# A layer norm's steps moved between the stages of a fused attention and gated-MLP kernel

## The chip, the cores and the metric

The kernel runs on one core of one Trainium2 chip. The metric is the device time of one execution in microseconds (us), as the median of several runs. A core has five engines that run side by side, each with its own queue in order: TensorE (PE; its weight loads are shown as PEld), VectorE (DVE), ScalarE (ACT), GpSimd (POOL) and SyncE (SP), which here issues nearly all transfers (DMA). Matmuls write to PSUM, all else lies in SBUF.

## The reference

The input x has 2048 rows of 640 in bf16. The output is x plus attention of the normed rows plus a gated MLP of the same normed rows:

```python
x = A_x
xn = _layernorm(x, axis=-1)
return x + _A_ref(xn, A_wqkv, A_wo) + _B_ref(xn, B_w_gate, B_w_up, B_w_down)
```

Attention has 32 heads of 20 and a causal window of 256 keys. The MLP has a hidden width of 1536:

```python
scores = jnp.einsum("bhqd,bhkd->bhqk", q, k) * (Dh ** -0.5)
mask = (idx[:, None] - idx[None, :] >= 0) & (idx[:, None] - idx[None, :] < W)
p = _softmax(jnp.where(mask[None, None], scores, -1e9), axis=-1)
o = jnp.einsum("bhqk,bhkd->bhqd", p, v)

h = _sigmoid(x @ w_gate) * (x @ w_up)
return h @ w_down
```

## The kernel before

The 2048 rows are cut into four chunks of 512 (`NCH`), each into four blocks of 128 (`SBC`). The order of all engines is written out by the program (`manual_schedule`). A loop over attention steps (lines 760 to 782) issues the scores of a step (line 530), their exponentials (535), their masks on GpSimd (542) or as a MIN on VectorE (547), and, when a pair of groups of heads is complete, the weighted sums of V (561). Between those steps, `Fill` pulls pieces of other work from a list of named parts (lines 732 to 748), as much as a planned cost allows. The parts run strictly one after the other:

- `qk<c>`: ten blocks of the projections of chunk c, first five for Q, then five for K (`g_qk`, 334). VectorE copies the Q blocks out of PSUM (338), ScalarE the K blocks (340). SP stores each block to DRAM (342) and loads it back, spread by heads (352).
- `v<c>`: eight projections of V (`g_v`, 364); half of them are copied by VectorE (373). In `v1`, SP also loads the output weights wo here, twelve transfers (226, 228, 231).
- `gu<c>`: the gate and up projections (`g_gu`, 454 and 461), each with a tanh on ScalarE (457) and a product on VectorE (465) that gives h.
- `out<c>`: for each of four blocks the down projection (475), the output projection of attention (482), and on VectorE the sum with the rows of x (486) in SBUF; SP loads those rows (492) and stores the result (497). For block 0 and block 1 the loads are issued when the part begins, for later ones when the block before them begins. A part `out<c>` may start only when the attention of chunk c is done. Between the down projection of block 0 and its output projection it does some gate and up pieces.

All these projections use one PSUM pool, `ps_d`, of four buffers handed out in turn, as do the sums of V (561), which come in pairs and which VectorE transposes out (573) and scales (581 to 589).

What this is about is the layer norm of chunks 1 to 3 and its transposition. `g_norms(c)` is a generator. Each call of `next` does one step, and steps without cost (`yield 0`) only let time pass: statistics of four blocks on VectorE (271, 277), after the fourth one the reciprocal root on GpSimd (285, 286), four empty steps (the first is reached in the same call as the root), then four norms on VectorE (295), each with a store of the normed block to DRAM by SP (306). After the fourth store, `load_quarters` has SP read the whole chunk back from DRAM in four transfers, rearranged (313). These wait for the four stores to have landed. `g_turns(c)` then has VectorE transpose the four blocks (317) into xnT, which all projections of the chunk read. The chunk's rows, the rearranged rows and the next chunk's rows all use one buffer (`xc`), so that the next chunk is loaded (159) after the transposes.

`mix(a, b, first, every, rest)` yields the pieces of a and, after piece number `first` and every `every` pieces from there, one step of b. With `rest` true, what is left of b follows at the end.

Before the change, chunk 2's four statistics steps lie in the K half of `qk1`, and the rest (empty steps, norms, stores, quarters, waiting, transposes) in `out0`, a step after every piece from the second. Chunk 3's statistics lie in `gu1b`, the rest in `out1`. The x of chunk 3 is loaded between `out0` and `qk2`.

Of the kernel before, what the change touches and what calls it, by code (L numbers as in the profile page):

```python
# [112 lines left out]
def kernel(  # L113
# [42 lines left out]
    def load_x(c):  # L156
        t = xp.tile([P, SBC, D], BF16, name="xc")
        xc[c] = t
        nc.sync.dma_start(out=t, in_=xr[:, c * SBC:(c + 1) * SBC, :])
# [40 lines left out]
    def load_gu(t, w, k, lo=0, hi=FS):  # L200
        nc.sync.dma_start(out=t[k][:, :, lo:hi],
                          in_=w.rearrange("(c p) f -> p c f", p=P)[:, :, k * FS + lo:k * FS + hi])
# [20 lines left out]
    def load_wo():  # L223
        by_head = A_wo.rearrange("(a b i d) n -> a i b d n", a=2, i=HG, d=DH)
        for i in range(HG):
            nc.sync.dma_start(out=wo[32 * i:32 * i + DH, 0:DC - 1, :], in_=by_head[0, i].rearrange("b d n -> d b n"))
        for i in range(HG):
            nc.sync.dma_start(out=wo[32 * i + DH:32 * i + 32, 0:DC - 1, :],
                              in_=by_head[1, i].rearrange("b d n -> d b n")[0:32 - DH])
        for i in range(HG):  # L230
            nc.sync.dma_start(out=wo[32 * i:32 * i + 32, DC - 1, :], in_=by_head[1, i][:, 32 - DH:DH, :])
# [84 lines left out]
    def turn_block(c, s):  # L316
        nc.vector.transpose(out=xnT[c][:, :, s * P:(s + 1) * P],  # L317
                            in_=xc[c][:, s, :].rearrange("p (j b f) -> p b j f", j=SBC, b=DC))

    def new_xnT(c):  # L320
        xnT[c] = xtp.tile([P, DC, CW], BF16, name="xnT")
# [5 lines left out]
    def proj_block(w, c, m):  # L327


        base = 0 if w == "q" else D  # L330
        ps = ps_d.tile([P, CW], FP32, name="pqk", tag="d")
        for d in range(DC):
            wt = wqkv[:, d, base:base + D].rearrange("p (k m) -> p m k", m=DC)
            nc.tensor.matmul(ps, lhsT=wt[:, m, :], rhs=xnT[c][:, d, :],  # L334
                             start=(d == 0), stop=(d == DC - 1))
        st = stp.tile([P, CW], BF16, name="st")
        if w == "q":
            nc.vector.tensor_copy(out=st, in_=ps)
        else:
            nc.scalar.copy(out=st, in_=ps)  # L340
        dst = scratch[w].rearrange("(h j) s -> h j s", j=32)
        nc.sync.dma_start(out=dst[:, 4 * m:4 * m + 4, :], in_=st)

    def spread(w, c, g0, g1):

        half, first = divmod(g0, GH)
        if first == 0:
            qk[w, c, half] = (qp if w == "q" else kp).tile([P, GH, CW], BF16, name=w + "T")
        src = scratch[w].rearrange("(a b p) s -> b p a s", a=2, p=P)
        for b in range(g0 // 2, g1 // 2):  # L350
            o = 2 * b - half * GH
            nc.sync.dma_start(out=qk[w, c, half][:, o:o + 2, :], in_=src[b])

    def new_v(c, s):
        v = vp.tile([P, 2, VH], BF16, name="v")
        vt[c * SBC + s] = v
        nc.gpsimd.memset(v[:, :, 0:16 * VW].rearrange("p k (h d) -> p k h d", d=VW)[:, :, :, DH:VW], 0.5)
        nc.gpsimd.memset(v[:, :, 16 * VW:], 0.0)
# [17 lines left out]
    def proj_v(c, s, hf, copy):  # L376
        copy_v(c, s, hf, project_v(c, s, hf), copy)

    MM = 216
# [21 lines left out]
    def g_turns(c, wait=0):  # L401
        for _ in range(wait):
            yield 0
        new_xnT(c)
        for s in range(SBC):
            turn_block(c, s)
            yield 0

    def g_qk(c):
        for w in "qk":  # L410
            for m in range(DC):
                proj_block(w, c, m)
                if c == 0 and w == "q" and m == 1:
                    load_x(1)
                if c == 0 and w == "q" and m == 3:
                    load_gu(wu, B_w_up, 0, FS // 2)
                if c and w == "k" and m == 1:
                    spread("q", c, 0, GH)
                yield 5 * MM
        if c == 0:  # L420
            spread("q", c, 0, 2)
            spread("k", c, 0, 2)
            spread("q", c, 2, 4)
            spread("k", c, 2, 4)

    def g_v(c):
        for s in range(SBC):
            new_v(c, s)
            for hf in range(2):
                proj_v(c, s, hf, nc.scalar.copy if hf else nc.vector.tensor_copy)  # L430
                if hf == 0:
                    yield 5 * 136
            if s == 0:
                spread("k", c, 0, 2)
                spread("k", c, 2, GH)
            if c == 1 and s == 2:
                load_wo()
            if s == 1:
                spread("q", c, GH, NG)
                spread("k", c, GH, NG)  # L440
            yield 5 * 136
# [4 lines left out]
    def part(w, d, f):  # L446
        k, first = divmod(f * P, FS)
        return w[k][:, d, first:first + P]

    def g_gu(c, f0, f1):  # L450
        for f in range(f0, f1):
            pg = ps_d.tile([P, CW], FP32, name="pg", tag="d")
            for d in range(DC):
                nc.tensor.matmul(pg, lhsT=part(wg, d, f), rhs=xnT[c][:, d, :],  # L454
                                 start=(d == 0), stop=(d == DC - 1))
            th = tp.tile([P, CW], FP32, name="th")
            nc.scalar.activation(out=th, in_=pg, func=TANH, scale=0.5)  # L457
            yield 5 * MM
            pu = ps_d.tile([P, CW], FP32, name="pu", tag="d")
            for d in range(DC):  # L460
                nc.tensor.matmul(pu, lhsT=part(wu, d, f), rhs=xnT[c][:, d, :],  # L461
                                 start=(d == 0), stop=(d == DC - 1))
            h = hp.tile([P, CW], BF16, name="h")
            ht[c, f] = h
            nc.vector.scalar_tensor_tensor(out=h, in0=th, scalar=1.0, in1=pu, op0=ADD, op1=MULT)  # L465
            yield 5 * MM
# [23 lines left out]
    def new_rows(c, s, name="rows", bufs=3, queue=nc.sync):  # L490
        rows = lnp.tile([P, D], BF16, name=name, bufs=bufs)
        queue.dma_start(out=rows, in_=xr[:, c * SBC + s, :])
        return rows
# [5 lines left out]
    def outp(c, s, ys, rows):  # L499
        for y, cut in zip(ys, HALVES):  # L500
            add_wo(c, s, y, cut)
        for y, cut in zip(ys, HALVES):
            add_x(y, cut, rows)
        store(c, s, rows)

    def g_out(c, between, ahead=()):
        nxt = new_rows(c, 0)
        for s in range(SBC):
            rows = nxt
            if s == 0:  # L510
                yield from ahead
            if s + 1 < SBC:
                nxt = new_rows(c, s + 1)
            ys = [ps_d.tile([P, CW], FP32, name=f"y{i}", tag="d") for i in range(2)]
            for y, cut in zip(ys, HALVES):
                yield from down(c, s, y, cut)
            if s == 0:
                yield from between
            outp(c, s, ys, rows)
            yield 10 * 136  # L520
# [115 lines left out]
    def mix(a, b, first, every=1, rest=True):  # L636

        for k, cost in enumerate(a):
            yield cost
            if k >= first and (k - first) % every == 0:  # L640
                yield next(b, 0)
        if rest:
            yield from b
# [75 lines left out]
    fill = Fill()  # L719
    GU = 10 * MM  # L720
    OUT = 4 * 34 * 136
# [5 lines left out]

    norms = {c: g_norms(c) for c in range(1, NCH)}
    first = itertools.chain(norms[1], g_turns(1, 8))
    second = itertools.chain(norms[2], g_turns(2, 5))  # L730
    third = itertools.chain(norms[3], g_turns(3, 5))
    fill.add("gu0a", mix(g_gu(0, 0, 4), first, 1, 1, False), 4 * GU)
    fill.add("gu0b", mix(g_gu(0, 4, 12), first, 0), 8 * GU)
    fill.add("wd", later(load_wd), 0)
    fill.add("x2", later(load_x, 2), 0)
    fill.add("qk1", mix(g_qk(1), second, 5, 1, False), 50 * MM)
    fill.add("v1", mix(g_v(1), g_gu(1, 0, 2), 1, 2), 40 * 136 + 2 * GU)
    fill.add("out0", mix(g_out(0, g_gu(1, 2, 3)), second, 1, 1), OUT + GU)
    fill.add("x3", later(load_x, 3), 0)
    fill.add("qk2", g_qk(2), 50 * MM)  # L740
    fill.add("v2", mix(g_v(2), g_gu(1, 3, 7), 0, 1), 40 * 136 + 4 * GU)
    fill.add("gu1b", mix(g_gu(1, 7, 12), third, 0, 2, False), 5 * GU)
    fill.add("out1", mix(g_out(1, g_gu(2, 0, 1)), third, 1, 1), OUT + GU)
    fill.add("qk3", g_qk(3), 50 * MM)
    fill.add("v3", mix(g_v(3), g_gu(2, 1, 5), 0, 1), 40 * 136 + 4 * GU)
    fill.add("gu2", g_gu(2, 5, 12), 7 * GU)
# [102 lines left out]
```

## Time and profile before

| | |
|---|---|
| median of 3 runs | 310.89 us (309.93 to 311.25) |
| the profiled execution | 310.85 us |
| its span, first to last instruction | 308.7 us |
| granted TensorE clock, mean | 1.000 |
| VectorE busy | 179.6 us |
| ScalarE busy | 198.3 us |
| GpSimd busy | 164.1 us |

The page's chain of work that ended last puts 87% on TensorE, 5% on VectorE and 4% on DMA. Its weightiest lines are the gate and up projections (16% each), Q and K (14%) and the down projection (14%). The stages around the change, in us from the span's start as their matmuls show in the timeline: `qk1` from 55.1, `v1` from 70.2, `out0` from 82.8, `qk2` from 108.2, `v2` from 122.1, `gu1b` from 139.8, `out1` from about 154. In a timeline each line has start, length, engine, line, operation, out<-in and how many were merged; in brackets stands how long the engine had been idle before, and what ended that.

A query of the busy time by stretches gives VectorE these shares (busy of length, us): 70 to 82: 9.06 of 12; 82 to 90: 7.67 of 8; 90 to 108: 10.30 of 18; 108 to 122: 9.15 of 14; 122 to 139: 10.07 of 17; 146 to 156: 8.75 of 10.

### The profile page before, as it was taken

The numbers are of one execution on the slowest core, as the hardware profiler recorded it, in microseconds if no ns is written. First come the engines' busy times: TensorE is split into PE (matmuls) and PEld (weight loads), VectorE is DVE, ScalarE is ACT, GpSimd is POOL, SyncE is SP. The second block draws the span as 40 slices with busy tenths as digits, with TensorE's granted clock in tenths as the row PEclk, the third lists the DMA queues.
The fourth block names the chain that finished last, engine by engine and source line by source line (L and its number), as shares of the span: only waits on it lengthen the run. The fifth ranks groups of instructions, "written<-read, shape, count | busy, mean of one in ns | idle before, by whom it ended". The sixth has DMA issues, their size and how long they took to land.

```text
span 308.7 us, 10027 instructions
## 1 busy us (share of the span) xinstructions
PE 300.8 (97%) x4309; PEld 168.1 (54%) x4344; DVE 179.6 (58%) x354; ACT 198.3 (64%) x196; POOL 164.1 (53%) x304
## 2 busy tenths in 40 slices
PE   7999999999999999999999999999999999999996
PEld 3654444555657655554456665554546665444775
DVE  4635657889684674485856755373643627372433
ACT  6933768688965647888655538978585557768100
POOL 3020667479874728576582827647383756657000
PEclk9999999999999999999999999999999999999999
DMA  7998969545746254630016313650000210000202
GB/s 208 365 292 266 319 212 287 150 137 151 213 150 114 61 180 130 196 115 0 2 46 148 91 57 92 196 171 0 4 0 4 67 41 23 2 2 2 87 23 65
DMA packets 40148, 36.04 MB, mean 117 GB/s; under 512 B 9000, under 2 KB 39848, under 8 KB 40104
## 3 DMA queue, kind: packets, MB, share of 16 engines
q1 hardware_dynamic: 39240, 34.63, 37.3%
q10 hardware_dynamic: 864, 0.77, 0.9%
q8 instruction: 34, 0.56, 0.8%
q14 instruction: 10, 0.08, 0.1%
HBM read 24.77 MB, written 10.62 MB: 115 GB/s over the span
## 4 chain that ended last, share of the span: by engine, by line
PE 87%; DVE 5%; DMA 4%; issue 1%; ACT 1%; SPq 1%; DVEq 0%
PE pg L454 16%; PE pu L461 16%; PE pqk L334 14%; PE y L475 14%; PE ps L530 8%; PE pv L364 8%; PE y L482 6%; PE acc L561 6%; DMA xc<-xr 2%; DMA xr<-xn 1%; DVE xnT L317 1%; DMA xc<-in_A_x_dram 1%; DVE h L465 1%; DVE on L585 1%; DVE stats L271 1%
## 5 line engine op out<-in xcount | busy, mean ns | idle before, releaser
L542 POOL TENSOR_SCALAR_AFFINE_SELECT pT<-pT 64x512 bf16<-64x512 bf16 (+1 forms) x252 | 152.5, 605 | 92.0 <-ACT pT L535 80.4
L535 ACT ACTIVATE pT<-ps 128x2048 bf16<-128x2048 f32 x75 | 140.8, 1877 | 60.3 <-PE ps L530 58.5
L465 DVE SCALAR_TENSOR_TENSOR h<-th,pu 128x512 bf16<-128x512 f32 x48 | 32.7, 682 | 52.1 <-PE pu L461 41.5
L461 PE MATMUL pu<-xnT,wu 128*128 128x512 bf16 x230 | 58.9, 380 | 0.7 <-issue 0.3
L454 PE MATMUL pg<-xnT,wg 128*128 128x512 bf16 x225 | 58.3, 380 | 1.2 <-issue 0.6
L475 PE MATMUL y<-wd,h 128*128 128x320 bf16 (+2 forms) x396 | 56.9, 296 | 0.3 <-DVE h L465 0.3
L334 PE MATMUL pqk<-xnT,wqkv 128*128 128x512 bf16 x190 | 45.1, 381 | 0.9 <-issue 0.4
L475 PEld LDWEIGHTS <-h 128*128 128x128 bf16 x396 | 36.6, 98 | 16.5 <-issue 2.2
L457 ACT ACTIVATE th<-pg 128x512 f32<-128x512 f32 x48 | 28.6, 596 | 15.3 <-PE pg L454 15.1
L454 PEld LDWEIGHTS <-wg 128*128 128x128 bf16 x240 | 22.2, 98 | 25.6 <-issue 2.0
L461 PEld LDWEIGHTS <-wu 128*128 128x128 bf16 x240 | 22.1, 98 | 25.4 <-issue 1.8
L334 PEld LDWEIGHTS <-wqkv 128*128 128x128 bf16 x200 | 22.5, 119 | 19.2 <-issue 1.7
L530 PE MATMUL ps<-qT,kT 20*64 20x320 bf16 (+4 forms) x1456 | 32.2, 259 | 0.3 <-issue 0.3
L573 DVE STREAM_TRANSPOSE t<-acc 128x512 f32<-128x512 f32 x32 | 21.1, 694 | 15.2 <-PE acc L561 15.2
L530 PEld LDWEIGHTS <-kT 20*64 20x64 bf16 x1456 | 15.9, 103 | 24.8 <-issue 22.3
L364 PE MATMUL pv<-wqkv,xnT 128*128 128x320 bf16 x160 | 26.0, 300 | 0.0
L482 PE MATMUL y<-wo,oc 128*128 128x320 bf16 (+2 forms) x165 | 24.2, 295 | 0.0
L486 DVE SCALAR_TENSOR_TENSOR rows<-y,rows 128x320 bf16<-128x320 f32 x30 | 14.1, 482 | 15.8 <-PE y L482 15.3
L373 DVE CAST v<-pv 64x320 bf16<-64x320 f32 x29 | 14.1, 486 | 11.2 <-PE pv L364 10.9
L561 PE MATMUL acc<-pT,v 64*32 64x320 bf16 (+4 forms) x1456 | 19.7, 252 | 0.0
L585 DVE TENSOR_TENSOR on<-t,rec 128x320 bf16<-128x320 f32 (+1 forms) x32 | 19.0, 594 | 1.1
L561 PEld LDWEIGHTS <-v 64*32 64x32 bf16 x1456 | 16.4, 91 | 5.8 <-DVE pT L547 1.3
(51 smaller groups left out, 175.8 us busy)
## 6 DMA issues: line engine op xcount, KB each, us to landing
qT<-sq SPq DMA_DIRECT2D x16, 256.0 KB
kT<-sk SPq DMA_DIRECT2D x16, 256.0 KB
sq<-st SPq DMA_DIRECT2D x20, 128.0 KB
sk<-st SPq DMA_DIRECT2D x20, 128.0 KB
out_dram<-rows SPq DMA_DIRECT2D x15, 160.0 KB
wg<-in_B_w_gate_dram SPq DMA_DIRECT2D x4, 480.0 KB
wu<-in_B_w_up_dram SPq DMA_DIRECT2D x4, 480.0 KB
xc<-in_A_x_dram SPq DMA_DIRECT2D x3, 640.0 KB
```

The costliest lines, as they stand in the source:

```text
L334: nc.tensor.matmul(ps, lhsT=wt[:, m, :], rhs=xnT[c][:, d, :], start=(d == 0), stop=(d == DC - 1))
L364: nc.tensor.matmul(ps[:, 0:HALF], lhsT=xnT[c][:, d, s * P:(s + 1) * P], rhs=wqkv[:, d, 2 * D + hf * HALF:2 * D + (hf + 1) * HALF], start=( ...
L454: nc.tensor.matmul(pg, lhsT=part(wg, d, f), rhs=xnT[c][:, d, :], start=(d == 0), stop=(d == DC - 1))
L457: nc.scalar.activation(out=th, in_=pg, func=TANH, scale=0.5)
L461: nc.tensor.matmul(pu, lhsT=part(wu, d, f), rhs=xnT[c][:, d, :], start=(d == 0), stop=(d == DC - 1))
L465: nc.vector.scalar_tensor_tensor(out=h, in0=th, scalar=1.0, in1=pu, op0=ADD, op1=MULT)
L475: nc.tensor.matmul(y[:, 0:cut[1] - cut[0]], lhsT=ht[c, f][:, s * P:(s + 1) * P], rhs=wd[:, f, cut[0]:cut[1]], start=(f == 0), stop=False)
L482: nc.tensor.matmul(y[:, 0:cut[1] - cut[0]], lhsT=oc[c, m][:, s * P:(s + 1) * P], rhs=wo[:, m, cut[0]:cut[1]], start=False, stop=(m == DC - 1))
L530: nc.tensor.matmul(ps[a * U:(a + 1) * U, i, col * U:(col + n) * U], lhsT=qk["k", kc, o // GH][32 * i:32 * i + DH, o % GH + a, kb * U:(kb + ...
L535: nc.scalar.activation(out=pt[:, :, 0:CW], in_=ps, func=EXP, scale=SCALE)
L542: nc.gpsimd.affine_select(out=view, in_=view, pattern=[[0, HG], [0, n], [sign, U]], compare_op=GE, fill=0.0, base=base, channel_multiplier ...
L561: nc.tensor.matmul(acc[32 * i:32 * i + 32, q * U:(q + n) * U], lhsT=vt[kb][a * U:(a + 1) * U, u, h * VW:h * VW + 32], rhs=pt[a * U:(a + 1) ...
```

## The change

The diff alters when steps of `g_norms` and `g_turns` of chunks 2 and 3 are issued. No operation is added, removed or resized, and the planned costs of the parts stay.

- Chunk 2: statistics stay in the K half of `qk1`. The rest of `g_norms(2)` moves from `out0` to `v1`, a step after each piece from the sixth. The transposes stay in `out0`, no longer chained behind the norms, from the eleventh piece and after every second one.
- Chunk 3: the statistics move from `gu1b` to the K half of `qk2`; the rest of `g_norms(3)` moves from `out1` to `v2`, a step after each piece from the second. The transposes stay in `out1`, from the sixth piece and after every second one.

```diff
     norms = {c: g_norms(c) for c in range(1, NCH)}
     first = itertools.chain(norms[1], g_turns(1, 8))
-    second = itertools.chain(norms[2], g_turns(2, 5))
-    third = itertools.chain(norms[3], g_turns(3, 5))
...
-    fill.add("qk1", mix(g_qk(1), second, 5, 1, False), 50 * MM)
-    fill.add("v1", mix(g_v(1), g_gu(1, 0, 2), 1, 2), 40 * 136 + 2 * GU)
-    fill.add("out0", mix(g_out(0, g_gu(1, 2, 3)), second, 1, 1), OUT + GU)
+    fill.add("qk1", mix(g_qk(1), norms[2], 5, 1, False), 50 * MM)
+    fill.add("v1", mix(mix(g_v(1), g_gu(1, 0, 2), 1, 2), norms[2], 5), 40 * 136 + 2 * GU)
+    fill.add("out0", mix(g_out(0, g_gu(1, 2, 3)), g_turns(2), 10, 2), OUT + GU)
     fill.add("x3", later(load_x, 3), 0)
-    fill.add("qk2", g_qk(2), 50 * MM)
-    fill.add("v2", mix(g_v(2), g_gu(1, 3, 7), 0, 1), 40 * 136 + 4 * GU)
-    fill.add("gu1b", mix(g_gu(1, 7, 12), third, 0, 2, False), 5 * GU)
-    fill.add("out1", mix(g_out(1, g_gu(2, 0, 1)), third, 1, 1), OUT + GU)
+    fill.add("qk2", mix(g_qk(2), norms[3], 5, 1, False), 50 * MM)
+    fill.add("v2", mix(mix(g_v(2), g_gu(1, 3, 7), 0, 1), norms[3], 1), 40 * 136 + 4 * GU)
+    fill.add("gu1b", g_gu(1, 7, 12), 5 * GU)
+    fill.add("out1", mix(g_out(1, g_gu(2, 0, 1)), g_turns(3), 5, 2), OUT + GU)
```

## The prediction

> **What bounds the kernel now.** I read the page first, then the timelines of TensorE (PE), VectorE (DVE) and the queue of SyncE (SP) around each place that the diff touches, then the chain of waits there. The page:
>
> ```profile
> span 308.7 us, 10027 instructions
> PE 300.8 (97%) x4309; PEld 168.1 (54%) x4344; DVE 179.6 (58%) x354; ACT 198.3 (64%) x196; POOL 164.1 (53%) x304
> PE   7999999999999999999999999999999999999996
> ```
>
> TensorE is busy 300.8 of 308.7 us, and what is missing lies in the first and the last slice. Two things follow. The change adds and takes away no TensorE work, so all it could win are the short waits of TensorE in the stages it touches. And a TensorE wait that it creates is paid in full, because no later idle time can swallow it. So each moved step is asked one question: does TensorE, in its fixed order, now wait for it? The place where I find such a wait is the start of "out0". SP's queue there, start and length of the issues:
>
> ```profile
> 79.31 4.34 SPq L228 DMA_DIRECT2D wo<-in_A_wo_dram  x4
> 83.69 2.83 SPq L231 DMA_DIRECT2D wo<-in_A_wo_dram  x4
> 86.56 0.93 SPq L492 DMA_DIRECT2D rows<-in_A_x_dram  x2
> 88.50 2.00 SPq L306 DMA_DIRECT2D xr<-xn  x3
> 91.21 0.34 SPq L497 DMA_DIRECT2D out_dram<-rows  x1
> 91.73 0.32 SPq L306 DMA_DIRECT2D xr<-xn  x1
> 95.73 1.92 SPq L313 DMA_DIRECT2D xc<-xr  x4
> 97.69 1.39 SPq L492 DMA_DIRECT2D rows<-in_A_x_dram  x1
> ```
>
> SP is busy with the loads of wo until 83.69 + 2.83 = 86.52. Then, at once, it issues the loads of the residual rows for blocks 0 and 1 of out0 (L492). The stores of chunk 2's normed rows (L306) and the quarters that read them back (L313) come after. What hangs on those rows, in TensorE's and VectorE's timelines:
>
> ```profile
> 89.12 1.53 PE L482 MATMUL y<-wo,oc 128*128 128x320 bf16 x10
> 90.49 0.98 PE L475 MATMUL y<-wd,h 128*128 128x320 bf16 x6
> ```
>
> ```profile
> 79.81 0.99 DVE L373 CAST v<-pv 64x320 bf16<-64x320 f32 x2 [1.85 <-PE pv L364]
> 81.63 0.69 DVE L465 SCALAR_TENSOR_TENSOR h<-th,pu 128x512 bf16<-128x512 f32 x1 [0.84 <-ACT pT L535]
> 87.91 1.08 DVE L295 TENSOR_SCALAR xn<-xc,mvs,rstds 128x640 bf16<-128x640 bf16 x2
> 90.07 1.12 DVE L486 SCALAR_TENSOR_TENSOR rows<-y,rows 128x320 bf16<-128x320 f32 x2
> ```
>
> The PSUM pool ps_d has four buffers that are handed out in turn. In out0 the order is y0, y1 (block 0), pg, pu, and then y0 of block 1, which is four further: it gets the buffer of block 0's y0, and that comes free when VectorE has added the rows (L486, 90.07). TensorE goes on with block 1 at 90.49, so there is no slack: whatever delays the rows of block 0 stops TensorE.
>
> **The change part by part.**
>
> (1) Chunk 2's norms, stores and quarters go from out0 into v1 (after its 8th to 11th of 12 pieces; six steps are left of the generator and seven visits remain, so all of it lies ahead of out0). For VectorE this costs nothing: two norms (0.6 us each) fit into the 1.85 us before 79.81 and two more around the 0.84 us before 81.63. They are done near 82; if this cover were gone, h would be 2.4 us later, which is not on TensorE's path before out1.
>
> For SP it is another matter. The generator of out0 starts when v1 has ended, so the queue becomes: wo, four stores, four quarters, and only then the rows of blocks 0 and 1. The quarters wait for the landing of the stores, and everything behind them waits too. Step by step:
> - SP is free at 86.52 as before. Four stores that wait for nothing take 0.32 + 0.06 each: the last is issued at 86.56 + 3 x 0.38 = 87.7.
> - From the last store to the first quarter: 91.73 to 95.73 = 4.0 us for chunk 2, and 1.8 us for chunk 3 (163.44 to 165.26). The chain of waits gives the first:
>
> ```profile
> 91.73 3.92 DMA xr<-xn
> 97.16 5.60 DMA xc<-xr
> ```
>
> Here four stores go out back to back behind wo's last loads, so it is nearer to chunk 2's row: I take 3.3, and 1.8 to 4.0 as bounds. First quarter at 91.0 (89.5 to 91.7), and the rows are issued at 91.0 + 1.92 + 0.05 = 93.0 in place of 86.56.
> - Landing. The last quarter of chunk 2 landed at 97.16 + 5.60 = 102.76, 7.0 us after the first was issued; for chunk 3 it was 6.6 (165.26 to 171.9). If the rows land behind the quarters, that is 91.0 + 7.0 = 98.0, at most 91.7 + 7.3 = 99.0. If they overtake them, the shortest landing of such a block in the trace (1.8) gives 93.0 + 1.8 = 94.8; with the earliest quarter 93.3. I take 98.0.
> [...]
> - VectorE needs 0.5 us for the first half of L486: TensorE resumes at 98.55 in place of 90.49. **Stall: 8.05 us.** VectorE stands still in the same time, being in order, and nothing behind it matters before TensorE goes on. The quarters have landed by then, so turning is no longer late.
>
> (2) What TensorE's clock does after 8 us without work. No idle of that length lies inside this trace. The nearest rows are the short gaps at 5 to 7 us (0.4 to 0.5 us idle, nothing slower behind them) and the start of the program, before which TensorE had done nothing:
>
> ```profile
> 0.83 4.43 PE L248 MATMUL pwarm<-const-bfloat16-1.0 128*128 128x512 bf16 x10 [0.83 <-PEq L833]
> ```
>
> Ten matmuls of 512 columns in 4.43 us, about 0.427 us apart; later five of them (L461) take 1.08 us, 0.216 apart. Bounds: 0, and 10 x 0.211 = 2.1 us (2.4 if the slow time were as long as 4.8). An idle of 8 us is nearer to the start: I take **2.0**.
> [...]
>
> (3) Chunk 2's turns, every second visit from the 11th of out0. They had waited 3.79 us for the quarters (102.89), and were so late that qk2's first matmul waited for L486: block 3 of out0 ends at 106.53 + 10 x 0.136 = 107.9, qk2 starts at 108.18. Gain 0.3.
>
> (4) Chunk 3's statistics go from gu1b into the K half of qk2 (five steps there, four blocks: 8 x 0.475 + 4 x 0.21, about 1.1 us a block). VectorE is idle for 3.92 us before v2's first copy at 123.02, and the K half's copies are ScalarE's. The input, issued at 109.79, has some 7 us before the first K block ends at 117 (chunk 2's was issued at 55.03 and nothing waited at 64.35). Cost nothing; without this cover v2's first copies would be up to 1 us late, which the four PSUM buffers take. In gu1b their going frees h:
>
> ```profile
> 156.13 1.67 PE L475 MATMUL y<-wd,h 128*128 128x320 bf16 x11 [0.29 <-DVE h L465]
> ```
>
> Gain 0.4 (idle 0.29, with modelled ends). POOL's two small operations for the root (0.23 + 1.04) move with them, where POOL holds masks that are needed some 10 us later.
>
> (5) Chunk 3's norms go into v2, after its 4th to 7th piece. The MIN on the probabilities (L547, 128.68) releases TensorE's sums at 129.11. One norm now stands between the copy that ends at 128.45 and it: 128.45 + 0.60 = 129.05, so 0.4 later. On SP the second half of chunk 2's q and k (127.55 to 129.56) waits some 3 us behind three stores; those scores come ten steps later. The quarters of chunk 3 block SP while nothing urgent is behind. In out1 a turn (0.84) stands before the first L486, where a norm (0.60) stood: 0.2. Loss 0.6.
>
> **Sum.** The profiled execution took 310.85 us (span 308.7 and 2.15 around it), the median is 310.89. 310.85 + 8.05 + 2.0 - 0.3 - 0.4 + 0.6 = **320.8 us**, 3% slower.
>
> **Rivals.**
> - The stall without a slow clock: 318.8. For it, the short gaps that cost no rate; against it, the start. 14%.
> - The rows overtake the quarters: they land at 94.8 to 96, TensorE resumes near 96, stall 5.5: 310.85 + 5.5 + 2.0 - 0.1 = 318.2, and 316.3 with no slow clock. For it, that transfers run on 16 engines side by side; against it, that chunk 2's quarters filled theirs for 5.6 us. 10%.
> - A longer hold: stores 4.0, landing 7.3, slow clock 2.4: resumption at 99.55, 310.85 + 9.05 + 2.4 - 0.1 = 322.2, and over it if four stores behind wo take longer than any in the trace. 8%.
> - Not slower: block 0's rows are in time. Then only the waits of (3) and (4) count, with (5) or without: 310.1 to 310.8. It decides by the first quarter: it would have to be out by about 90 - 7 = 83, which SP, at wo until 86.52 (4.34 us for four issues that wait for earlier landings), can't do unless wo's loads go faster than before. 6%.
>
> **How the numbers follow.** Forecast 62%: 320.8. From the cases, 316.5 to 323.0 leaves out the last rival, part of the overtaking and the tail of the long hold. Differences under 0.5% (1.6 us) can't be told from no change here. Of the 6%, two go to faster by more than that and four to no change; slower 94%.
>
> **What would show it.** In the changed profile SP's L492 loads of out0 stand behind four L313 and start near 93; a VectorE wait at L486 for the rows and a TensorE gap of 6 to 9 us near 90.5; matmuls of 512 columns 0.427 us apart behind it; no wait of L317 for the quarters; no L475 wait for h near the end of gu1b; L295 of chunk 3 in v2. I am wrong if TensorE passes from block 0 to block 1 of out0 without a gap, or if y0 of block 1 doesn't have to wait for L486.

## The result and the profile after

The changed kernel took 316.08 us in the median (312.88 to 318.28, six runs), the kernel before 310.71 us. The ratio is 1.015 with an interval of 1.012 to 1.019. So it is slower, as forecast, but by 1.5% and not by 3%, and just outside the range. (The ratios here and below leave out executions far above the fastest of their kernel; some of the change's own slower outcomes are among them, so the medians can lie further apart than a ratio says.)

The page of the changed kernel, in an execution of 316.76 us:

```profile
span 314.6 us, 10022 instructions
PE 302.6 (96%) x4309; PEld 169.5 (54%) x4344; DVE 179.1 (57%) x354; ACT 198.3 (63%) x196; POOL 164.0 (52%) x304
PE   7999999999995999999999999989999999999996
PEclk9999999999996999999999999999999999999999
```

The counts of matmuls and of the other engines' instructions are those of before. One slice of TensorE has a hole, and the same slice has a lower granted clock. SP's queue around that slice:

```profile
82.83 2.83 SPq L231 DMA_DIRECT2D wo<-in_A_wo_dram  x4
85.77 1.87 SPq L306 DMA_DIRECT2D xr<-xn  x4
89.99 1.91 SPq L313 DMA_DIRECT2D xc<-xr  x4
91.94 0.96 SPq L492 DMA_DIRECT2D rows<-in_A_x_dram  x2
```

The queue is as the prediction wrote it: wo, four stores, the wait for their landing, four quarters, and only then the rows. VectorE waits for them:

```profile
97.14 0.89 DVE L486 SCALAR_TENSOR_TENSOR rows<-y,rows 128x320 bf16<-128x320 f32 x2 [7.79 <-DMA rows<-in_A_x_dram]
```

TensorE, though, passes from block 0 to block 1 of out0 without a stop. It stops one step later:

```profile
88.84 1.53 PE L482 MATMUL y<-wo,oc 128*128 128x320 bf16 x10
90.21 0.98 PE L475 MATMUL y<-wd,h 128*128 128x320 bf16 x6
91.12 0.42 PE L530 MATMUL ps<-qT,kT 20*64 20x256 bf16 x16
91.47 2.62 PE L475 MATMUL y<-wd,h 128*128 128x320 bf16 x18
97.68 2.72 PE L561 MATMUL acc<-pT,v 64*32 64x320 bf16 x96 [3.59 <-DVE rows L486]
100.92 2.58 PE L482 MATMUL y<-wo,oc 128*128 128x320 bf16 x10
```

All 24 down projections of block 1 run at once (90.21 to 94.1). The next that needs PSUM buffers are the sums of V, and these wait for L486. In the profile of before they followed block 1 directly:

```profile
91.76 2.62 PE L475 MATMUL y<-wd,h 128*128 128x320 bf16 x18
94.31 1.29 PE L561 MATMUL acc<-pT,v 64*32 64x320 bf16 x96
```

Behind the wait, 96 sums take 2.72 us where they took 1.29, and ten output projections 2.58 where they took 1.53. The stretches of time say why; the columns are the stretch, its length, the busy times, and then PEclk, DMA share and GB/s:

```profile
94.10:97.70 3.60, 0.02 (x4) 0.02 (x4) 0.56 (x2) 0.00 (x0) 0.00 (x0) 0.80 0.47 99
97.70:103.10 5.40, 5.40 (x129) 3.54 (x130) 3.19 (x6) 1.88 (x1) 0.01 (x1) 0.50 0.22 64
103.10:106.90 3.80, 3.80 (x50) 2.62 (x49) 3.26 (x8) 1.29 (x1) 2.80 (x4) 1.00 0.27 86
```

TensorE's granted clock is 0.50 until 103.1, and 1.00 from there. Where the 5.9 us between the two spans (308.7 and 314.6) arose can be read from the start of the same TensorE instruction in both traces. The lead or lag of the changed kernel steps as follows:

| place | step, us |
|---|---|
| first transposes (rows of chunk 0 landed a little earlier) | -0.30 |
| wait of the sums of V for the rows, in out0 | +3.68 |
| halved clock behind it | +2.64 |
| start of qk2, no wait for L486 | -0.24 |
| end of gu1b, no wait for h | -0.59 |
| in v3, TensorE idle with no wait that the trace shows (0.30 us before, 1.10 after) | +0.79 |

They add up to 5.98, where the spans lie 5.9 us apart. The first step is no effect of the change: the traces of all the other kernels have it too, with -0.2 to -0.4 us, so the profiled execution of the kernel before was late there.

### The profile page after: what moved, and what is told of

Same layout as the page of the kernel before. It is cut to its first block, busy times and chain, and to the rows that moved or that the text cites. A ratio compares the mean times of both kernels' runs of the same rounds, so it can differ in the third digit from the quotient of the medians.

```text
span 314.6 us, 10022 instructions
## 1 busy us (share of the span) xinstructions
PE 302.6 (96%) x4309; PEld 169.5 (54%) x4344; DVE 179.1 (57%) x354; ACT 198.3 (63%) x196; POOL 164.0 (52%) x304
## 4 chain that ended last, share of the span: by engine, by line
PE 90%; DMA 3%; DVE 3%; issue 2%; SPq 1%; ACT 1%; DVEq 0%
PE pg L454 16%; PE pu L461 16%; PE y L475 15%; PE pqk L334 14%; PE ps L530 8%; PE pv L364 7%; PE y L482 7%; PE acc L561 6%; DMA rows<-in_A_x_dram 2%; DMA xr<-xn 1%; DMA xc<-in_A_x_dram 1%; SPq L313 1%; DVE on L585 1%; PE pt L302 0%; DVE v L373 0%
## 5 line engine op out<-in xcount | busy, mean ns | idle before, releaser
L486 DVE SCALAR_TENSOR_TENSOR rows<-y,rows 128x320 bf16<-128x320 f32 x30 | 14.4, 487 | 30.1 <-PE y L482 22.0
L482 PE MATMUL y<-wo,oc 128*128 128x320 bf16 (+2 forms) x165 | 25.3, 304 | 0.0
L561 PE MATMUL acc<-pT,v 64*32 64x320 bf16 (+4 forms) x1456 | 21.1, 260 | 3.6 <-DVE rows L486 3.6
L561 PEld LDWEIGHTS <-v 64*32 64x32 bf16 x1456 | 17.2, 94 | 9.9 <-DVE rows L486 4.2
L482 PEld LDWEIGHTS <-oc 128*128 128x128 bf16 x165 | 16.0, 100 | 6.9 <-DMA xr<-xn 0.2
```

What stands on the lines that cost most here:

```text
L482: nc.tensor.matmul(y[:, 0:cut[1] - cut[0]], lhsT=oc[c, m][:, s * P:(s + 1) * P], rhs=wo[:, m, cut[0]:cut[1]], start=False, stop=(m == DC - 1))
L561: nc.tensor.matmul(acc[32 * i:32 * i + 32, q * U:(q + n) * U], lhsT=vt[kb][a * U:(a + 1) * U, u, h * VW:h * VW + 32], rhs=pt[a * U:(a + 1) ...
```

## The experiments

Each was timed beside the kernel before on its chip: 310.39 us for the rows first, the rows between and the two parts alone; 310.91 us for the changed kernel again, the filled wait and ScalarE's queue; 311.03 us for the other three. "Rows" are the loads of the residual rows of blocks 0 and 1 of out0. Where an experiment adds lines, the line numbers behind them move by a few. The theory to test: their place on SP's queue is the whole loss, first as a wait and then as a clock that the wait has lowered. The rivals: VectorE crowded by norms in v1 and v2, the part of chunk 3, full DMA engines, and slow matmuls with another cause.

**The rows first.**

```diff
                 load_wo()
+                early.extend(new_rows(0, k) for k in range(2))
...
-        nxt = new_rows(c, 0)
+        nxt = early.pop(0) if c == 0 else new_rows(c, 0)
...
-                nxt = new_rows(c, s + 1)
+                nxt = early.pop(0) if early else new_rows(c, s + 1)
```

> The changed kernel, with out0's loads of the rows of blocks 0 and 1 issued right behind the loads of wo, ahead of the four stores of the norms. Theory A (the rows, held on SP's queue behind the stores' landing and the quarters, are the whole loss): no VectorE wait for rows, no TensorE gap near 94, clock 1.000, and the two small gains stay (0.24 at qk2's start, 0.7 at the end of gu1b): about 309.9 us, ratio 0.995 to 0.999. Theory B (the norms in v1 or the spread transposes crowd VectorE, and the rows are only where it shows): a wait of several us stays near 94, over 313 us.

309.95 us (309.43 to 310.80, 12 runs), ratio 0.999 with 0.997 to 1.000: theory A. The sums of V follow block 1 with no wait, as before the change:

```profile
91.49 2.62 PE L478 MATMUL y<-wd,h 128*128 128x320 bf16 x18
94.03 1.29 PE L564 MATMUL acc<-pT,v 64*32 64x320 bf16 x96
```

Everything else of the change is in this kernel, so norms in v1 and v2 and spread transposes cost nothing that can be measured. In the trace the two gains stay (0.29 at qk2, 0.58 in gu1b).

**The rows between the stores and the quarters.** The same, with the line `early.extend(...)` ahead of `load_quarters(2)` in place of behind `load_wo()`.

> The same two row loads, issued between the fourth store and the quarters. Theory A1 (the wait for the stores' landing and the quarters are what holds the rows): rows issued near 87.7, landed by 91.5, before TensorE needs the PSUM buffers at 94: about 309.9 us, as with the rows first. Theory A2 (the stores' own transfers matter as well): rows land after 94, a TensorE gap of 1 us or more, over 311.5 us.

310.16 us (309.38 to 311.83), ratio 1.000 with 0.998 to 1.002: theory A1. Here VectorE does wait for the rows, and TensorE doesn't notice:

```profile
88.72 0.93 SPq L496 DMA_DIRECT2D rows<-in_A_x_dram  x2
```

```profile
91.42 0.89 DVE L490 SCALAR_TENSOR_TENSOR rows<-y,rows 128x320 bf16<-128x320 f32 x2 [2.10 <-DMA rows<-in_A_x_dram]
```

The rows came 2.7 us after their issue, and L486's sum is over near 92.3; the buffers are wanted at 94.0. So this place has about 1.7 us to spare, which the prediction had put at none.

**Chunk 3's part alone**, chunk 2 as before:

> The part of the change on chunk 3 alone; chunk 2 as before. Theory A: no loss in it; the wait for h at the end of gu1b goes (0.7 us) and the MIN that comes 0.2 us later holds nobody: about 310.1 us, ratio 0.996 to 1.000. Theory B (norms ahead of the MIN in v2, and the late spreads of q and k, cost TensorE time): 311.2 us or more.

310.22 us (309.48 to 310.99), ratio 1.000 with 0.999 to 1.002: the time alone can't tell a gain of 0.6 us. The trace can: the 24 down projections at the end of gu1b run without the wait for h, and the start of v2 shows no new one. Theory A by the trace, undecided by the time.

```profile
153.45 3.43 PE L475 MATMUL y<-wd,h 128*128 128x320 bf16 x24
```

In this execution the quarters of chunk 2, in their old place, landed by 101.4 (102.8 in the profile of before), and qk2 started without a wait. Chunk 2 is here as in the kernel before, so the 0.3 us of the prediction's step (3) are a wait that this order of chunk 2 doesn't always have.

**Chunk 2's part alone**, chunk 3 as before:

> The part on chunk 2 alone; chunk 3 as before. Theory A: the whole loss is here, without the 0.7 us won in gu1b: between 313.5 us (clock not lowered) and 318 us (lowered for about 7 us), median near 316.5, ratio 1.012 to 1.022. Theory B (half of the loss or more is chunk 3's): under 313 us.

316.84 us (311.77 to 319.57, seven runs), ratio 1.010 with 1.006 to 1.014. The median is near its forecast; the ratio lies just under its forecast, and the spread is wider. Theory A: both halves of the loss are here, a wait of 3.56 us and the halved clock behind it, and gu1b still has its wait for h of 0.29 us:

```profile
93.90:97.60 3.70, 0.17 (x2) 0.00 (x0) 0.52 (x2) 0.00 (x0) 0.00 (x0) 0.83 0.54 107
97.60:103.20 5.60, 5.57 (x129) 3.60 (x130) 3.23 (x6) 1.88 (x1) 0.16 (x1) 0.50 0.20 61
```

**The changed kernel again**, to see its spread:

> The changed kernel again. If the loss is a fixed wait of 3.6 us and a lowered clock that depends on where the wait falls: times in steps that go with the granted clock, about 312.9 at 1.000, 315 at 0.995, 317 at 0.989. If the spread has another cause: times that don't go with the clock.

317.32 us (313.29 to 319.00). With the six runs of the first result there are twelve, and they fall into three groups by the mean granted clock:

| granted clock | times, us |
|---|---|
| 1.000, 0.999 | 312.88, 313.29 |
| 0.995, 0.994 | 314.68, 314.72, 315.40 |
| 0.989 | 316.76, 317.22, 317.24, 317.42, 318.28, 318.39, 319.00 |

With the lowered clock at 0.50, as in the profiled execution, a mean of 0.995 over 313 us is an estimated 0.005 x 313 / 0.5 = 3.1 us at half clock, 0.989 is 6.9 us. The two runs at full clock lie some 2.3 us above the kernel before, which is the wait net of the gains. The other groups lie about 2 and about 4 to 6 us above these two. The clock can't be all of that: 3.1 us at half clock cost at most 1.6 us of work and 6.9 us at most 3.4 (2.64 in the first profile). And the wait isn't fixed, as this expectation had it. In the profile of this run (317.42 us) SP needed 3.60 us to issue the four quarters, where it had needed 1.91, the rows were there at 98.65, and TensorE stood for 4.55 us:

```profile
99.19 2.72 PE L561 MATMUL acc<-pT,v 64*32 64x320 bf16 x96 [4.55 <-DVE rows L486]
```

So part of the difference between the groups is the length of the wait, and the kernel before alone spreads from 309.64 to 312.42 us on the same chip. How much each adds in the executions without a profile isn't known.

**The wait filled with matmuls that compute nothing used:**

```diff
+            if pair == (1, 0):
+                idle = ps_s.tile([P, HG, CW], FP32, name="idle", tag="ps")
+                for k in range(15):
+                    nc.tensor.matmul(idle[:, 0, :], lhsT=ones[:, 0:P], rhs=ones, start=(k == 0), stop=(k == 14))
             pv(*pair, parts.pop(pair))
```

> The changed kernel, with 15 matmuls of 512 columns (3.2 us at full clock) that compute nothing used, put where TensorE otherwise stands idle near 94. Theory C (the idleness lowers the clock, and that is the second half of the loss): granted clock 1.000 in every run, the wait for the rows stays, time 312.5 to 313.3 us with a spread under 1 us. Theory D (the matmuls behind the wait are slow for another reason, as VectorE's or ScalarE's backlog): 315 us or more, as the changed kernel.

317.58 us (314.07 to 319.70): the time was missed by 4 us, and the granted clock was 0.994 or 0.995 in three of the six runs. The other three took 314.07, 315.56 and 317.15 us, so a lowered clock isn't all of the rest. The trace splits this. At the place itself theory C holds. The wait for the rows is there, and longer (VectorE gets them at 98.97; before it TensorE had also waited 0.87 us for wo, until 90.39), and the granted clock is 1.00 behind it:

```profile
95.00:98.10 3.10, 3.10 (x16) 1.31 (x14) 0.00 (x0) 0.00 (x0) 0.00 (x0) 1.00 0.93 197
99.50:104.00 4.50, 4.41 (x139) 3.30 (x140) 3.49 (x8) 1.88 (x1) 0.31 (x1) 1.00 0.26 76
```

But in v3, where this kernel differs in nothing, TensorE stood for 3.1 us with no wait that the trace shows, and now the clock fell there, to half from 210.23 to 213.65: five gate matmuls in 1.81 us, where 1.24 is usual.

```profile
210.37 1.01 PE L461 MATMUL pu<-xnT,wu 128*128 128x512 bf16 x2 [3.10 <-issue]
212.50 1.81 PE L454 MATMUL pg<-xnT,wg 128*128 128x512 bf16 x5
```

**The rows first, with the same 15 matmuls**, as a control for that:

> The kernel with the rows first, where nothing waits, with the same 15 unused matmuls. They cost 15 x 0.216 = 3.2 us of TensorE. Theory F (30 more instructions shift the place where TensorE stands without a next instruction near 206, and that made up the rest of the time of the kernel with the stall filled): 315 us or more, with a gap of 2 us or more in v3 in the trace. Theory G (they shift nothing): about 313.2 us.

316.70 us (313.26 to 318.44): theory F in the trace and in four of six runs; the two others, 313.26 and 313.57 us, are what theory G forecast. In the profiled execution there is no wait in out0 and the 15 matmuls cost 3.28 us; the rest comes from the same gap in v3 and the lowered clock behind it (0.989 in the mean):

```profile
207.86 1.01 PE L464 MATMUL pu<-xnT,wu 128*128 128x512 bf16 x2 [3.18 <-issue]
```

So the time of the kernel with the wait filled can't be used as a measure of the clock's share; the granted clock in its trace can. What the gap in v3 waits for isn't settled by these runs. In all nine traces with a gap there of over 0.2 us, TensorE goes on 1.3 to 1.5 us after a transfer of 16 KB has landed on the queue that the page calls "instruction": landed at 203.85 and on at 205.34 before, 209.89 and 211.31 in the changed kernel, 209.03 and 210.37 with the wait filled, 206.52 and 207.86 here. So late instructions are likely, but no run changes their supply alone. The gap also varies without any added instruction: 0.30 us before, 1.10 after, hardly any (0.09) in the second profile of the changed kernel, 1.66 with ScalarE's queue, which comes next. The two kernels with 30 more instructions had 3.1 and 3.2 us, in one profiled execution each.

**The rows issued by ScalarE**, at the same place of the program (`queue=nc.scalar` for both loads):

> The changed kernel, with the same two row loads at the same place of the program, but issued by ScalarE. Theory A (what holds them is SP, which waits in order for the stores' landing): issued near 83 to 88, landed before 93, no TensorE gap, about 309.9 us. Theory E (the DMA engines are full with wo, stores and quarters): the rows still land after 94, TensorE gap over 1 us, over 311.5 us.

310.54 us (309.68 to 311.94), ratio 1.000 with 0.998 to 1.002: theory A. ScalarE issues them from 83.1, while SP is still at wo, and L486 waits for its matmul and not for the rows:

```profile
83.08 1.68 ACTq L492 DMA_DIRECT2D rows<-in_A_x_dram  x2
```

```profile
89.79 0.49 DVE L486 SCALAR_TENSOR_TENSOR rows<-y,rows 128x320 bf16<-128x320 f32 x1 [0.49 <-PE y L482]
```

The transfers are those of the changed kernel, stores and quarters among them; it is SP's order that held the rows.

**The rows between the second and the third quarter:**

```diff
         for q in range(4):
+            if (c, q) == (2, 2):
+                early.extend(new_rows(0, k) for k in range(2))
```

> The changed kernel, with the two row loads issued between the second and the third quarter. They are issued some 1 us earlier than in the changed kernel (near 91 in place of 91.9), and have half of the quarters ahead of them. Theory R (transfers of one queue are served about in the order of their issue, so the rows wait for the quarters ahead of them): landed near 94.5, 2.5 us earlier than the 97.1 of the changed kernel; TensorE gap at most 1 us, clock 1.000, 310 to 311.5 us. Theory S (the quarters ahead don't matter, only the time of issue does): landed about 1 us earlier, near 96; gap 2 to 3 us, over 312 us.

315.57 us (311.08 to 316.46), ratio 1.011 with 1.005 to 1.016. Gap and time are those of theory S. The rows were issued 0.65 us earlier than in the first profile of the changed kernel, and VectorE had them 0.65 us earlier, as if half of the quarters ahead of them made no difference:

```profile
90.39 0.85 SPq L316 DMA_DIRECT2D xc<-xr  x2
91.29 0.96 SPq L495 DMA_DIRECT2D rows<-in_A_x_dram  x2
92.29 0.96 SPq L316 DMA_DIRECT2D xc<-xr  x2
```

```profile
96.49 0.89 DVE L489 SCALAR_TENSOR_TENSOR rows<-y,rows 128x320 bf16<-128x320 f32 x2 [7.05 <-DMA rows<-in_A_x_dram]
```

As a rule theory S doesn't hold, though. In the second profile of the changed kernel the rows were issued at 95.31, 3.37 us later than in the first, and VectorE had them only 1.51 us later (98.65 against 97.14). And by the packets it is theory R for most. Of the rows' 256 packets of 1280 bytes, 241 were done between 92.5 and 94.5, mostly between the packets of the two halves of the quarters, and the last 15 by 96.5. Service was about in the order of issue, and the landing was set by a small tail. What two quarters fewer ahead of the rows are worth stays open. TensorE's wait was 2.85 us, and the clock fell in five of six runs all the same (0.989 to 0.995 in the mean).

**The transposes close together**, in the kernel with the rows first (`g_turns(2), 10, 1` and `g_turns(3), 5, 1`):

> The kernel with the rows first, with the transposes of chunks 2 and 3 after every piece in place of every second. Theory A (the wait of 0.3 us at qk2's start came from quarters that landed late, not from transposes that stood close): no difference to the rows first, about 310.0 us, and no wait at qk2's start. Theory T (it is the distance between them that takes the wait away): the 0.3 us come back in the trace, at qk2's start or at the first sum of out1.

310.22 us (309.63 to 311.21), ratio 0.998 with 0.996 to 1.000: theory A. qk2 starts without a wait (107.79, right behind block 3). The distance between the transposes does nothing that shows here. That fits late quarters as the cause of the small wait, as does chunk 3's part alone, where they landed 1.4 us earlier and qk2 didn't wait.

## Why the prediction was right, and where it was wrong

- **SP's queue**: right, and near in numbers. Last store at 87.3 (forecast 87.7), first quarter at 89.99 (forecast 91.0, bounds 89.5 to 91.7), rows issued at 91.94 (93.0), rows there 7.0 us after the first quarter (7.0), at 97.0 (98.0). The kernels with the rows first, between and on ScalarE's queue show that this is the cause.
- **Where TensorE stops**: wrong, and this is the step that failed. The prediction, like the description of the kernel ahead of it, said that ps_d's buffers are "handed out in turn", so that y0 of block 1 gets the buffer of block 0's y0 and TensorE stops at 90.49. Block 1 ran through from 90.21 to 94.1 while L486 had not begun, which the prediction itself had named as the sign of being wrong. The first to want block 0's buffers were the sums of V, at 94.1, and the trace shows both: the sums into the first accumulator start at 97.68, when the first half of L486 is done (97.64), those into the second wait for its second half, until 98.08. In the profile of before, block 1 started just as block 0's rows were added (90.49 and 90.07), and I read a dependence into two times that only lay close together. Which buffers block 1 got isn't in the trace; those of pg and pu, which the program gives back first, would fit. The stall was 3.6 us (94.1 to 97.68) where 8.05 were forecast: 3.6 less by this step, 0.9 less because the rows came earlier. The buffers aren't all that hangs on the rows. The MIN on the probabilities of these sums stood behind L486 on VectorE (97.94, against 93.89 before). The first sum after the start that waits for VectorE again came 1.5 us behind it, at half clock. So with free buffers TensorE would, by an estimate from these times, have stopped some 0.8 us later and still waited until the MIN was done at 98.35. No run shows this.
- **The clock**: right that TensorE goes on at a lower clock behind the stall (0.50 granted), and it took less idleness than forecast. Forecast 2.0 for a stall of 8; measured 2.64 in the profiled execution, after 3.6 us of idleness, 2.78 in the second one, and nothing in the two executions at full clock. I expected one amount, and the twelve runs lie in three groups: about none, and by the estimate from their mean clocks 3.1 and 6.9 us at half. The mean of 0.80 over 94.1 to 97.7 stands for 0.20 x 3.6 / 0.5 = 1.4 us at half, so the clock was down from about 96.3, 2.2 us after the last matmul. The clock records in the traces say it exactly: at half from 96.28 to 103.11, which is 6.83 us, and from 210.23 to 213.65, which is 3.42, in the kernel with the wait filled.
- **Norms on VectorE in v1**: right, no cost (rows first).
- **Chunk 3**: the gain in gu1b was 0.59 us where 0.4 was forecast (the expectations put it at 0.7). The forecast loss of 0.6 did not come. The MIN was late by 0.24 us against its place before (134.70, where 128.68 plus a lag of 5.78 is 134.46), and the sums behind it started on time.
- **qk2's start**: 0.24 us, forecast 0.3, but a wait that the kernel before doesn't always have.
- **The sum** with the measured terms: 310.85 + 3.7 + 2.6 - 0.2 - 0.6 = 316.35 us, and 316.8 with the two steps of the table that no part of the change explains (-0.30 and +0.79). The profiled execution took 316.76.

## What to carry to other kernels

When a transfer that waits is moved ahead on a queue that issues in order, list what stood behind its new place and when each of those is needed: here two loads of 160 KB, of which the diff says nothing, cost all of it, and moving them ahead of the quarters on the same queue, or to another engine's queue, undid the loss. A buffer dependence should be shown by a wait in the trace, not by two times that lie close together. A stall of 3 to 4 us on TensorE (3.59 us here, and 2.64 more at the lowered clock) should be priced with the clock that follows it, as a set of outcomes and not as one number.

## What the runs showed of the hardware

- The granted clock fell 2.2 us after the last matmul (94.1 to 96.28), and stayed at half for 6.83 us although TensorE was at work from 97.7. The kernel with a wait of 2.85 us in its profile lost clock in five of six runs (0.989 to 0.995); a gap of 1.66 us in v3, with ScalarE's queue, lowered nothing (1.000).
- In three traces the clock record gives the time of the fall: 2.2 us after the end of the last matmul in the changed kernel (96.28), 3.0 us with the wait filled (210.23) and 2.4 us with the rows first and the same matmuls (207.05). That isn't one time. No run shows what sets it, and an execution whose clock didn't fall at such a wait has no trace here.
- One program with a wait at one place gives times around 313, 315 and 317 to 319 us, at mean granted clocks of 0.999 to 1.000, 0.994 to 0.995 and 0.989. The wait was 3.59 us in one profile and 4.55 in another.
- Thirty more instructions on TensorE, far ahead, went with a gap of 3.1 to 3.2 us in v3, where kernels without them had at most 1.66 us. In both of their traces the clock fell in that gap (210.23 and 207.05).
